# A gated linear attention and a bilinear feed-forward on one core: state products of both halves in turn, prefix sums as 64x64 tiles, and new orders

## The chip, the cores and the metric

The kernel runs on one core of a Trainium2 chip. A core has five engines with a queue of instructions each: TensorE (PE) multiplies matrices and writes to PSUM, VectorE (DVE) and ScalarE (ACT) work element by element on SBUF and PSUM, GpSimd (POOL) on SBUF alone, and SyncE (SP) issues DMAs; POOL and ACT issue DMAs too. Each queue runs in order, and the queues wait for each other through semaphores. In the profile PEld is TensorE's loading of stationary operands. The metric is the device time in microseconds (us), the median of the runs shown.

## The reference, cut to what matters

```python
state = np.zeros((B, H, D, D))                       # 4 batch rows, 8 heads, D = 48
for t in range(S):                                   # 768 tokens
    state = alpha[:, :, t, :, None] * state + np.einsum('bhd,bhe->bhde', k[:, :, t], v[:, :, t])
    y[:, :, t] = np.einsum('bhd,bhde->bhe', q[:, :, t], state)
x = y.transpose(0, 2, 1, 3).reshape(B * S, H * D)    # 3072 x 384
out = ((x @ w_a) * (x @ w_b)) @ w_out                # 384 -> 1536 -> 384
```

The recurrence decays the state by a gate per key channel. Over a block of tokens it turns into products of matrices: with b the product of the gates from the start of the block, keys divided by b and queries multiplied by b, the scores of queries and keys under a causal mask give what stays within the block, and the state that comes in gives the rest. The logarithms of the gates are summed by a matmul with a triangular matrix of ones, so b is the exponential of a prefix sum.

## The kernel before, in words

The work is six chunks. Chunk c holds two of the four batch rows (u = 0, 1) and 256 tokens (segment c // 2). Two neighbouring tokens lie on one of the 128 partitions, so the partitions hold 128 pairs. The pairs fall into two halves of 64 (g = 0, 1), that is of 128 tokens each, and the state is carried from one half to the next: S0 comes in, Sm lies between the halves, S0 of the next segment goes out.

Per chunk these steps follow each other. In brackets stand their short names in PROGRAM.

- Loads of alpha, k, q and v by DMA (ld).
- The logarithm of alpha on ACT (ln, logs), and the sum of each pair of tokens on DVE (l2, pairs, line 561).
- The prefix sums. Chunk 0 takes them straight from the logarithms in fp32 (B, cum_both). Chunks 1 to 5 split the pair sums into a high part, rounded for the fast fp32 mode (H, high, line 598), and what is left (L, low, line 604), and multiply both by the 128x128 triangle utr (A2, cum2, line 628): two matmuls of 384 columns per batch row. The triangle has zeros between the halves, so each half has sums of its own.
- The exponential of the sum and of its negative on ACT (E, line 656); products that scale keys and queries, on DVE (mk, mq, line 666); before them a product that brings the first token of a pair to its own level (lv, line 642, on POOL or DVE).
- A transpose of the scaled keys and queries, by PE and an eviction in chunks 0 and 1 (C and Ce, lines 707 to 715), by a DMA from SP afterwards (T, line 718). The decay over a half is taken from the last row of the exponentials by a pair of small DMAs (dr and dl), in chunks 0 and 1 by PE (dk and de).
- The scores, 64x64 tiles of 128 columns (D, line 786), masked on DVE (M), or copied on ACT and masked in place on DVE (Mc and Mm).
- The products of keys and values for the state, 64x64 tiles of 48 columns. K takes one half (line 744): its tiles lie in the same 64 rows of the array and take turns over its two column halves. K2 lets both halves alternate (line 757). The state is then updated on DVE (k).
- The output of attention: what is carried (SB and SA) and the inner block (Y), both at line 810, evicted as xT (X).
- The feed-forward for the chunk: a and b (line 864, 512 columns for the whole chunk, or 256 for one half of its columns), an eviction of a on ACT (as), the product with b on DVE (pr, line 878), the output matmul in two halves of six (o, line 886; oc at the very end, line 897), its eviction (ot) and the store (st).

PSUM has eight banks; the last figure of a PE step is its bank, and two-bank tiles name the first. A bank comes free when its eviction or product is done. PROGRAM is one list, written out, in which the steps of several chunks are interleaved. Each step goes to its engine's queue in the order of the list, so the list sets the order of every queue, SP's and POOL's DMAs among them. The feed-forward of one chunk fills PE while the next chunk's prefix sums, exponentials and transposes run on other engines. Two steps, fill and warm, are matmuls on zeros that only keep PE running. In the list, two further functions (cross, cum_quads) exist without being used.

Of the kernel before, what the change touches and what calls it, by code (L numbers as in the profile page):

```python
# [41 lines left out]
0: cz 1 v P
2: ld a * P
0: as 1 1; a 6 * 4; as 3 1; pr 1 1
1: ra 0
0: a 0 1 0; a 2 1 7; a 8 * 1; b 3 1 2; pr 5 1; k 1 1 V
1: H 1 V; H 0 S
0: as 6 *
1: L 1 V
0: b 2 1 3; a 11 * 5; pr 3 1  # L50
1: L 0 V
0: a 7 * 6
1: ld v 1 P
0: as 11 *; b 6 * 2; as 2 1; pr 6 *; b 11 * 7; a 10 * 4
1: ra 1
0: as 0 1; pr 2 1
1: v 0 V
0: pr 11 *; as 7 *
1: lv 0 k P; A2 0 2
2: ld k * P  # L60
0: b 0 1 0
1: A2 1 5
0: as 8 *; b 7 * 3
1: lv 0 q V
0: pr 0 1
2: ld q * P
1: E 1 i; E 0 b
0: pr 7 *
1: E 1 b; E 0 i; mq 0 V
0: b 10 * 6; b 9 * 1; a 9 * 7; as 9 *; as 10 *  # L70
1: mk 0 V
0: b 8 * 0
1: dk * 5
0: pr 8 *; pr 10 *; pr 9 *
1: C 0 1 3; C 0 0 4
0: o 3 0 0
1: Ce 0 1 S; de *; Ce 0 0 V; K2 0 7 3; D 0 0 4; k 0 0 V; D 0 1 1; Mc 0 0; lv 1 k P; SB 0 6; M 0 1
# [12 lines left out]
1: Ce 1 0 V; v 1 V  # L90
2: l2 * V
0: ot 0 S; o 1 1 -
2: ra 0
1: SA 0
0: ot 1 S
2: H * S
1: D 1 0 1; K 1 0 3
2: lv 0 k P
1: M 1 0; Y 0
0: o 2 1 -  # L100
1: X 0 S; C 1 1 5
0: ot 2 S
1: a 5 0 6
2: L * V
1: Ce 1 1 V
2: lv 1 k P
1: a 3 0 1; k 1 0 V; as 3 0; a 1 0 0; as 5 0; b 1 0 7; b 3 0 2; as 1 0
2: A2 1 1
1: pr 3 0
2: ra 1  # L110
3: ld k * P
1: pr 1 0; SB 1 5
2: E 1 i
1: D 1 1 3; K 1 1 2; M 1 1
2: lv 1 q P; lv 0 q P; E 1 b
1: a 11 0 0
2: A2 0 7
1: as 11 0; b 11 0 1
2: E 0 i
1: b 5 0 0; pr 11 0  # L120
2: E 0 b
1: a 4 0 4; pr 5 0; a 0 0 3
2: dr
1: a 6 0 1; k 1 1 V; as 4 0; as 0 0; a 2 0 0; b 4 0 7
2: mk 1 V
1: as 6 0; b 6 0 3; pr 6 0; a 7 0 1; b 0 0 2; pr 4 0; b 7 0 4; pr 0 0; a 9 0 3; as 9 0
2: mq 1 V
1: as 2 0; SA 1; Y 1; as 7 0
2: T 1
1: b 9 0 2; X 1 S; pr 7 0; a 8 0 3; pr 9 0; b 2 0 0; as 8 0  # L130
2: v 1 S
1: b 8 0 1; pr 2 0; a 10 0 4; b 10 0 2
3: lv 0 k P
1: a 0 1 0
2: mq 0 V
1: as 10 0; a 9 1 5; as 0 1; pr 10 0; a 5 1 6
4: ld a * P
1: b 5 1 7
3: ln *
1: b 0 1 3; pr 8 0; a 2 1 0  # L140
2: dl
3: lv 1 k P
1: as 5 1; pr 0 1; a 1 1 2; b 1 1 4; as 1 1; pr 5 1; as 9 1; b 9 1 3; pr 1 1; as 2 1; a 8 1 6
2: mk 0 V
1: a 4 1 7; b 2 1 1
2: v 0 S
1: as 4 1; pr 9 1; a 11 1 2; b 11 1 0; b 4 1 5; pr 2 1; b 8 1 3; pr 4 1; as 8 1; pr 8 1
3: l2 * V
1: a 3 1 4
2: T 0  # L150
1: as 11 1; a 7 1 1; b 3 1 6
0: st 3 Y
1: o 2 0 5; a 10 1 7; as 7 1
3: ld q * Y
1: pr 11 1; as 3 1
0: st 1 Y
1: as 10 1; pr 3 1
2: D 1 0 3; K * 0 1; Mc 1 0; D 1 1 6; k * 0 V
1: a 6 1 0; b 7 1 2
3: ra 1  # L160
2: Mc 1 1
1: pr 7 1
5: ld a * Y
1: b 10 1 3; o 2 1 -; as 6 1
3: ra 0
0: st 0 Y
1: b 6 1 4; ot 2 S; pr 10 1
2: Mm 1 0 V; D 0 0 2; K * 1 1
3: H * V
1: pr 6 1; o 3 0 0  # L170
2: Mc 0 0; k * 1 V; Mm 1 1 V; SB 0 4; SB 1 6
3: L * V
2: D 0 1 2
# [12 lines left out]
2: X 0 S
3: E 0 b
1: o 0 1 -
3: lv 0 q V; E 1 b; E 0 i; mk 0 V
1: ot 3 S  # L190
3: E 1 i
2: b 5 * 6; b 3 * 4; a 4 * 5; a 5 * 7
1: ot 0 S
3: mq 1 V
2: a 3 * 2; a 2 * 1
3: dr
2: a 1 * 3; as 5 *; b 0 * 7; as 3 *; b 1 * 0; as 1 *
# [36 lines left out]
2: b 10 * 5; as 9 *; a 10 * 6; b 7 * 3; pr 9 *; as 10 *; o 0 0 0; pr 7 *; pr 10 *
3: D 1 1 6; D 1 0 1
4: lv 1 k P
3: M 1 1
2: o 0 1 -
3: Mc 1 0
5: ld q * P  # L240
3: Mm 1 0 V; SB 0 3
2: ot 0 S
3: SB 1 1; D 0 1 5
4: lv 1 q V; A2 0 0
2: o 2 0 7
3: Mc 0 1
4: ra 0; lv 0 k V
5: ln *
4: E 0 b
3: Mm 0 1 V  # L250
2: o 3 0 6
3: Mm 0 0 V
5: lv 1 k P
4: lv 0 q P
5: ld v * P
3: Y 1; SA 0; Y 0; SA 1
2: o 3 1 -
3: X 0 S; X 1 V
2: o 2 1 -
4: mq 0 V; A2 1 2  # L260
2: ot 2 S
3: a 2 * 5
5: l2 * V
3: b 4 * 3
4: E 1 b; E 0 i; E 1 i
3: b 3 * 4; a 4 * 7; b 2 * 2
4: v 1 S
3: as 2 *
4: dr
# [12 lines left out]
5: lv 0 q V
3: pr 8 *
4: mq 1 V
5: lv 0 k V
3: as 0 *
5: ra 1
3: a 3 * 1; a 5 * 3; b 0 * 7; a 9 * 6; as 5 *; pr 5 *; a 7 * 3; a 11 * 5; pr 0 *; as 9 *; as 3 *; as 1 *
4: T 1
3: b 9 * 6; b 1 * 1  # L290
5: lv 1 q V
3: pr 9 *; a 6 * 2; pr 3 *; as 11 *; pr 1 *; as 6 *
4: K * 0 0; D 0 0 4
5: L * V
3: as 7 *; b 11 * 6; b 6 * 7; pr 11 *; a 10 * 1; pr 6 *
4: Mc 0 0
2: o 1 0 5
3: as 10 *
4: k * 0 V; D 1 0 3; D 1 1 6; D 0 1 1
5: v 1 S  # L300
4: Mc 1 0; M 1 1
5: A2 0 0
2: o 1 1 -
4: SB 0 6; Mc 0 1; Mm 0 0 V; SB 1 3
2: ot 1 V
5: A2 1 2
3: b 7 * 1
5: E 1 i; E 1 b; E 0 b
3: b 10 * 5
4: Mm 0 1 V; Mm 1 0 V  # L310
3: pr 7 *; o 1 0 2
5: mk 1 V
3: pr 10 *; o 2 0 1
5: mq 1 V
4: Y 1; SA 0
5: dr
2: st 3 Y
# [91 lines left out]
def kernel(  # L409
# [84 lines left out]
    def const_utr(eng):  # L494
        ENG[eng].tensor_copy(utr, ut)
# [542 lines left out]
```

## Time and profile before

| what | value |
| --- | --- |
| median of 3 runs | 195.31 us (194.95 to 195.92) |
| profiled execution, its time | 195.05 us |
| profiled execution, its span | 193.3 us |
| PE busy | 187.9 us, 97% |
| DVE busy | 132.9 us, 69% |
| ACT busy | 106.3 us, 55% |
| POOL busy | 51.4 us, 27% |
| DMA bytes | 29.40 MB, 152 GB/s over the span |

The time of an execution holds the span, from the first instruction to the last, and 1.75 us around it. Busy times are shares of the span. In the rows by slice each digit is the busy share of a fortieth of the span in tenths. The chain of work that ended last is followed back from the last instruction, at each step to what released it; its shares tell on which engine the time went. A row of the timeline gives start, length, engine, line, operation, output and inputs, shape and count; rows of the same kind that follow each other are merged. PE's matmuls overlap in the pipeline, so what one costs the queue is the distance between starts.

### The profile page before, as it was taken

How to read it: one execution, taken by the hardware profiler on the slowest of the kernel's cores; microseconds unless marked ns; L12 is line 12 of the kernel's file. 1: busy time of each engine (PE TensorE's matmuls, PEld its weight loads, DVE VectorE, ACT ScalarE, POOL GpSimd, SP SyncE). 2: the span in 40 equal slices, each digit the busy share in tenths (PEclk: the TensorE clock that was granted, in tenths of full speed). 3: DMA queues.
4: the chain of work that ended last, by engine and by line, in shares of the span. 5: the costliest groups of instructions: out<-in, count | busy, mean ns of one | idle time of the engine just before them, and what ended most of it. 6: DMA issues, size and time to landing. Idle time of an engine off the chain costs nothing.

```text
span 193.3 us, 5977 instructions
## 1 busy us (share of the span) xinstructions
PE 187.9 (97%) x2582; PEld 117.7 (61%) x2582; DVE 132.9 (69%) x221; ACT 106.3 (55%) x197; POOL 51.4 (27%) x69
## 2 busy tenths in 40 slices
PE   7989999999999999999999999999999999999993
PEld 3878875566888876644557544656455644455562
DVE  2498787988898879579787877896585525543311
ACT  4638785656859786645547775853462353431311
POOL 8999649260927003600007400000000000000000
PEclk9999999999999999999999999999999999999999
DMA  5999999999976989999598999006950100000342
GB/s 144 268 215 226 244 244 226 261 249 266 243 211 116 187 210 303 120 272 191 110 288 194 143 227 113 0 4 79 183 127 0 44 3 0 0 0 0 131 148 93
DMA packets 57034, 29.40 MB, mean 152 GB/s; under 512 B 47560, under 2 KB 54600, under 8 KB 57008
## 3 DMA queue, kind: packets, MB, share of 16 engines
q0 software_dynamic: 19056, 15.73, 44.2%
q1 hardware_dynamic: 37808, 13.19, 31.2%
q8 instruction: 20, 0.33, 0.7%
q10 hardware_dynamic: 144, 0.10, 0.2%
q14 instruction: 6, 0.05, 0.1%
HBM read 25.98 MB, written 4.74 MB: 159 GB/s over the span
## 4 chain that ended last, share of the span: by engine, by line
PE 91%; DMA 3%; POOL 2%; ACT 1%; DVE 1%; issue 1%; POOLq 0%; DVEq 0%
PE psum L864 48%; PE psum L886 24%; PE psum L810 7%; DMA a_t<-in_alpha_dram 3%; PE psum L786 3%; PE psum L628 2%; PE psum L707 2%; PE psum L744 2%; PE psum L897 1%; PE psum L687 1%; PE psum L588 1%; PE psum L589 1%; PE psum L757 1%; POOL v_t L547 0%; ACT la L554 0%
## 5 line engine op out<-in xcount | busy, mean ns | idle before, releaser
L864 PE MATMUL psum<-xT,wb_t 128*128 128x512 bf16 (+1 forms) x270 | 56.0, 337 | 0.0
L864 PE MATMUL psum<-xT,wa_t 128*128 128x512 bf16 (+1 forms) x270 | 55.5, 337 | 0.0
L886 PE MATMUL psum<-wo_t,prod 128*128 128x384 bf16 x276 | 49.5, 326 | 0.0
L864 PEld LDWEIGHTS <-wa_t 128*128 128x128 bf16 x270 | 25.9, 98 | 19.7 <-issue 0.2
L864 PEld LDWEIGHTS <-wb_t 128*128 128x128 bf16 x270 | 25.7, 98 | 20.0 <-issue 0.6
L886 PEld LDWEIGHTS <-prod 128*128 128x128 bf16 x276 | 26.0, 98 | 18.3 <-issue 0.5
L901 ACT ACTIVATE ot<-psum 128x384 f32<-128x384 f32 (+1 forms) x20 | 9.5, 480 | 19.5 <-PE psum L886 15.8
L642 POOL TENSOR_TENSOR k_t<-k_t,a_t 128x384 f32<-128x384 f32 x8 | 9.6, 1200 | 37.3 <-DMA k_t<-in_k_dram 35.9
L795 ACT ACTIVATE m<-psum 128x1024 bf16<-128x1024 f32 x15 | 15.1, 1022 | 4.6 <-PE psum L786 4.3
L791 DVE TENSOR_TENSOR m<-psum,mask 128x1024 bf16<-128x1024 f32 x9 | 10.9, 1216 | 3.2 <-PE psum L786 3.2
L554 ACT ACTIVATE la<-a_t 128x1536 f32<-128x1536 f32 (+2 forms) x9 | 9.5, 1055 | 5.6 <-DMA a_t<-in_alpha_dram 5.5
L845 ACT ACTIVATE xT<-psum 128x768 bf16<-128x768 f32 x8 | 6.5, 810 | 8.8 <-PE psum L810 8.7
L666 DVE TENSOR_TENSOR QKp<-k_t,invb 128x768 bf16<-128x768 f32 x10 | 9.4, 951 | 2.4 <-issue 1.5
L799 DVE TENSOR_TENSOR m<-m,mask 128x1024 bf16<-128x1024 bf16 x15 | 10.7, 736 | 0.1
L810 PE MATMUL psum<-m,vx 64*64 64x128 bf16 x576 | 10.2, 217 | 0.2 <-DVE m L799 0.2
L666 DVE TENSOR_TENSOR QKp<-q_t,beta 128x768 bf16<-128x768 f32 x10 | 10.0, 998 | 0.1
L786 PE MATMUL psum<-kqT 64*64 64x128 bf16 x384 | 9.7, 219 | 0.3 <-DVE kqT L715 0.2
L810 PEld LDWEIGHTS <-vx 64*64 64x64 bf16 x576 | 8.9, 107 | 1.0 <-issue 0.8
L547 POOL DMA_DIRECT2D v_t<-in_v_dram x8 | 8.4, 1051 | 0.1
L786 PEld LDWEIGHTS <-kqT 64*64 64x64 bf16 x384 | 6.7, 106 | 2.3 <-issue 1.9
L810 PE MATMUL psum<-kqT,Sm 64*64 64x128 bf16 x144 | 7.6, 220 | 0.1
L642 POOL TENSOR_TENSOR q_t<-q_t,ra 128x384 f32<-128x384 f32 x4 | 4.1, 1026 | 13.4 <-ACT m L795 13.1
(264 smaller groups left out, 281.1 us busy)
## 6 DMA issues: line engine op xcount, KB each, us to landing
out_dram<-ot SPq DMA_DIRECT2D x23, 192.0 KB, 2.9
a_t<-in_alpha_dram POOLq DMA_DIRECT2D x3, 768.0 KB, 13.8
q_t<-in_q_dram POOLq DMA_DIRECT2D x3, 768.0 KB, 8.7
k_t<-in_k_dram POOLq DMA_DIRECT2D x2, 768.0 KB, 11.7
v_t<-in_v_dram POOLq DMA_DIRECT2D x4, 384.0 KB, 6.2
k_t<-in_k_dram SPq DMA_DIRECT2D x2, 768.0 KB, 6.3
a_t<-in_alpha_dram POOLq DMA_DIRECT2D x3, 384.0 KB, 9.1
q_t<-in_q_dram POOLq DMA_DIRECT2D x3, 384.0 KB, 13.6
```

Of the source, the lines that this page charges most:

```text
L547: eng.dma_start(out=t[:, us, hs].rearrange("p b h r d -> p (b h) (r d)"), in_=src[ch.b0 + us.start:ch.b0 + us.stop, hs, ch.s * 2 * C:(ch.s ...
L554: nc.scalar.activation(out=ch.la[:, us, hs].rearrange("p b h r d -> p (b h r d)"), in_=ch.a[:, us, hs].rearrange("p b h r d -> p (b h r d) ...
L642: eng.tensor_mul(x, x, by)
L666: eng.tensor_mul(QKp[ch.c % 2][:, u, j, :, hs, :D], src[:, u, hs].rearrange("p h r d -> p r h d"), f)
L786: nc.tensor.matmul(s2[g * HC:(g + 1) * HC, r, p, rk, :], lhsT=ch.kqT[u][rs, 1, rk, 2 * h + p, g * HC:(g + 1) * HC], rhs=queriesT(ch, u, 2 ...
L791: nc.vector.tensor_mul(m.rearrange("p r a k s -> p (r a) (k s)"), ch.s2[u, h].rearrange("p r a k s -> p (r a) (k s)"), maskn(4))
L795: nc.scalar.activation(out=m.rearrange("p r a k s -> p (r a) (k s)"), in_=ch.s2[u, h].rearrange("p r a k s -> p (r a) (k s)"), func=AF.Copy)
L799: eng.tensor_mul(x, x, maskn(4))
L810: nc.tensor.matmul(y[c * DP:(c + 1) * DP, g, j // 2 * C:(j // 2 + 1) * C], lhsT=lhsT, rhs=rhs, start=(g, c) not in begun, stop=False, skip ...
L864: nc.tensor.matmul(p, lhsT=(wa_t, wb_t)[w][:, kk, f * 128:(f + 1) * 128], rhs=ch.xT[:, kk, us, :], start=(kk == 0), stop=(kk == KT - 1))
L886: nc.tensor.matmul(op, lhsT=ch.prod[:, f, at:at + C], rhs=wo_t[:, f, :], start=(f == 0), stop=(f == NFF - 1))
L901: nc.scalar.activation(out=o_, in_=i_, func=AF.Copy)
```

## The change

1. Prefix sums of chunks 2 to 5 (AQ, cum_quads in place of A2, cum2). The pair sums of batch row 1 are written to the other 64 partitions, half 0 to partitions 64 to 127 and half 1 to 0 to 63 (l2s, pairs_crossed). The sums are kept as three bf16 parts: the upper 16 bits of the fp32 sum, read in place (top), the upper 16 bits of what is left, and those of what is left again (R, rest, two differences on DVE). Twelve matmuls of 64x64 with the bf16 triangle utb and 384 columns follow: three parts by two rows by two halves, the rows in one bank each, and the four of one part in the four quarters of the array. H and L are gone for these chunks; chunk 1 keeps A2.
2. State products (K2, state_pe_both). The function now takes the batch rows of each half apart. K2 is used for both rows of chunk 1, one at a time, and for chunks 2 and 3 whole; chunk 0 and the last segment (chunks 4 and 5, where only the first half's update is needed) keep K.
3. New orders. PROGRAM is written anew throughout: which feed-forward step stands between which steps of the next chunk, the banks, the engine of some evictions, casts and level products (lv), and the order of loads and stores. In the start the fill of the first q and k tile goes from POOL to DVE, the identity is made ahead of the triangle, and SP loads k ahead of q.
4. Layouts. The decay tile and the row it comes from have the half as an inner index. Three further functions (decay_quads, decay_quads_exp, turn_quads with its eviction) are added and not used.

The diff, cut to its core (the steps of PROGRAM that the text speaks of, then the functions):

```diff
-1: A2 0 2
-1: A2 1 5
...
-2: L * V
...
-2: A2 1 1
...
-2: A2 0 7
...
-2: D 1 0 3; K * 0 1; Mc 1 0; D 1 1 6; k * 0 V
...
-2: Mm 1 0 V; D 0 0 2; K * 1 1
...
-3: A2 1 3
...
-4: lv 1 q V; A2 0 0
...
-4: mq 0 V; A2 1 2
...
-5: A2 0 0
...
-5: A2 1 2
...
+1: A2 0 7
...
+1: A2 1 7
...
+1: Mc 0 0; K2 0 0 7 0
...
+1: v 1 V; D 1 0 3; Ce 1 1 S; K2 1 1 6 0; Y 0; SA 0
...
+2: l2 0 V
+1: X 0 S; a 3 0 1; Mc 1 1
+2: l2s 0 P; l2s 1 P
+1: a 2 0 3; a 4 0 4
+2: R 0
+1: k 1 1 V; as 4 0
+2: ra 1
+1: as 3 0; b 4 0 7
+0: o 2 1 -
+1: as 2 0
+0: ot 2 S
+1: pr 4 0
+2: R 1; lv 1 q P
+1: b 3 0 6; b 2 0 7; a 5 0 2; pr 3 0; b 5 0 3; as 5 0; b 1 0 5; a 1 0 1; pr 5 0; pr 2 0; a 7 0 2; as 1 0; pr 1 0
+2: AQ 3
+1: SB 1 6
...
+2: K2 * * 0 7; D 1 1 3; D 1 0 5
...
+3: AQ 2
...
+3: K2 * * 4 6
...
+2: ot 2 S; o 0 1 -
+4: AQ 0; E 0 b; E 0 i
+3: SA 0; Y 0; SA 1
+4: E 1 b
+3: Y 1
+5: l2s 1 V
+4: mq 0 V; mk 0 V
+3: X 0 S; X 1 S
+2: o 3 0 2; o 3 1 -
+4: T 0
+3: a 5 * 3
+4: E 1 i; v 0 S
+3: a 9 * 0
+2: ot 3 S
+3: b 5 * 6; a 6 * 5; as 5 *
...
+3: a 0 * 1
+4: mk 1 V
+3: a 1 * 2
+4: D 0 0 3
...
+5: AQ 6; E 0 i; E 0 b; mk 0 V
...
-    def cross(ch, eng):
...
+    def pairs_crossed(ch, g, eng):
...
+        x = ch.la[g * HC:(g + 1) * HC, 1]
+        eng.tensor_add(ch.l2[(1 - g) * HC:(2 - g) * HC, 1], x[:, :, 0, :], x[:, :, 1, :])
+
+    def top(t):
+        return t.bitcast(BF16).rearrange("p b h (d t) -> p b (h d) t", t=2)[:, :, :, 1]
+
+    def rest(ch, n):
+        name = ("lh", "ll")[n]
+        t = wk.tile([C, 2, H, D], F32R, name=name, bufs=1)
+        setattr(ch, name, t)
+        x, hi = (ch.l2, top(ch.l2)) if n == 0 else (ch.lh.bitcast(F32), top(ch.lh))
+        nc.vector.tensor_sub(t.bitcast(F32).rearrange("p b h d -> p b (h d)"), x.rearrange("p b h d -> p b (h d)"), hi)
 
     def cum_quads(ch, i):
         p = wide(i)[:, :, :H * D]
         for u in range(2):
             ch.pf[u, 0, H] = p[:, u]
-        for t in (ch.lh, ch.ll):
+        for n, x in enumerate((top(ch.l2), top(ch.lh), top(ch.ll))):
             for u in range(2):
                 for g in range(2):
                     gs, to = slice(g * HC, (g + 1) * HC), slice((g ^ u) * HC, ((g ^ u) + 1) * HC)
-                    nc.tensor.matmul(p[to, u], lhsT=utr[gs, gs], rhs=t[gs, u].rearrange("p h d -> p (h d)"), start=(t is ch.lh), stop=(t is ch.ll))
+                    nc.tensor.matmul(p[to, u], lhsT=utb[gs, gs], rhs=x[gs, u], start=(n == 0), stop=(n == 2))
...
-    def state_pe_both(ch, us, t0, t1):
+    def state_pe_both(ch, us0, us1, t0, t1):
         i = ch.c % 2
-        for u in range(us.start, us.stop):
-            for g, tag in enumerate((t0, t1)):
+        pair = []
+        for g, us_, tag in ((0, us0, t0), (1, us1, t1)):
+            for u in range(us_.start, us_.stop):
                 ch.kv[u, g] = bank(tag)
...
+            pair.append([(u, p, rk, r) for u in range(us_.start, us_.stop) for p in range(P2) for rk in range(2) for r in range(2)])
+        for both in zip(*pair):
+            for g, (u, p, rk, r) in enumerate(both):
+                gs = slice(g * HC, (g + 1) * HC)
+                e = (u * P2 + p) * D
+                nc.tensor.matmul(ch.kv[u, g][r * DP:(r + 1) * DP, e:e + D], lhsT=QKp[i][gs, u, 1, rk, 2 * p + r, :], rhs=vxs[i][gs, u, rk, 2 * p + r, :D], start=(rk == 0), stop=(rk == 1))
```

More of the change, by code (lines that the diff above doesn't have):

```diff
@@ new lines @@
+0: pr 3 1
+1: Mc 0 0; K2 0 0 7 0
+0: o 1 0 6
+1: mk 1 V; M 0 1
+0: o 3 0 4; o 1 1 -; ot 1 S; c3 P
+3: ld a * P
+0: cs 1 0 P; o 3 1 -
+1: k 0 0 V; k 0 1 V; Mm 0 0 V; SB 0 1; C 1 0 3; C 1 1 7
+0: ot 3 S; o 0 1 -
+1: Ce 1 0 V
+2: ln *
+1: v 1 V; D 1 0 3; Ce 1 1 S; K2 1 1 6 0; Y 0; SA 0
+0: ot 0 V
+1: k 1 0 V; D 1 1 6
+0: o 2 0 5
+1: M 1 0
+2: l2 0 V
[9 more added lines that the diff above has]
+0: ot 2 S
@@ new lines @@
+2: SB 0 5
+1: pr 7 1
+3: R 0
+2: D 0 0 2
+1: ot 2 V
+2: Mm 1 0 V
+1: o 3 1 -
+2: Mc 0 0; SB 1 0; D 0 1 2
+3: R 1
+1: ot 3 S
+2: SA 0
+1: o 0 0 4
+0: cs 0 0 P
+2: Mc 0 1
+4: ln *
+3: ld q * Y; ld k * Y
+2: k * 1 V
+3: AQ 2
+2: Y 1; SA 1; Mm 0 1 V; Mm 0 0 V; Y 0; X 0 S
+3: E 0 b
+4: l2 0 V
+2: X 1 V
+1: o 0 1 -
+2: b 1 * 6; a 1 * 5
+3: E 1 b
+4: ld k * Y
+3: E 1 i
+1: ot 0 S
+3: E 0 i
+4: l2s 0 P
+2: a 0 * 0; b 0 * 1; as 0 *; as 1 *
+3: lv 0 k P; lv 0 q P
+2: a 5 * 7
+1: st 3 Y
+2: a 7 * 4
+4: l2s 1 P
@@ new lines @@
+2: a 2 * 5
+3: lv 1 q V; mq 1 V; lv 1 k V
+2: pr 1 *
+3: dr
+2: pr 0 *
+3: mk 0 V
+4: ld q * Y
+0: st 2 Y
+2: as 5 *; a 6 * 6; b 6 * 2; as 7 *
+3: mq 0 V
+2: b 9 * 4; b 7 * 0
+1: st 2 Y
+3: dl
+4: R 0
+2: b 5 * 7
+1: o 1 0 3
+2: a 9 * 1; pr 7 *; as 6 *
+3: T 0
+2: pr 6 *
+4: ra 0
+2: pr 5 *; a 11 * 6
+3: mk 1 V
+2: as 9 *; a 3 * 0
+4: lv 0 k V; lv 0 q V; R 1
+2: as 2 *
+1: o 1 1 -
+2: as 11 *; a 8 * 5; b 11 * 2; a 4 * 7; b 2 * 1
+3: T 1
+1: ot 1 V
+2: pr 9 *; as 8 *; pr 11 *; pr 2 *; b 8 * 3; b 4 * 5; as 4 *
@@ new lines @@
+5: ld v * P; lv 1 k P
+3: a 11 * 1
+5: ra 0
+3: as 3 *; pr 8 *; as 11 *; a 7 * 0
+4: D 1 0 3; K * 0 5
+5: lv 0 q P
+3: pr 3 *; as 7 *
+5: v 1 V
+4: k * 0 V
+5: R 1
+4: D 1 1 6; D 0 1 1; Mc 1 0; Mc 1 1; M 0 1
+2: o 1 0 0; o 1 1 -
+3: a 10 * 7; b 11 * 3
+4: SB 1 4
+2: ot 1 S
+3: as 10 *
+4: Mm 1 0 V
+3: pr 11 *
+4: SB 0 1
+5: AQ 6; E 0 i; E 0 b; mk 0 V
+3: b 10 * 0; b 7 * 3
+4: Mm 1 1 V
+5: mq 0 V
+3: o 2 0 6; pr 7 *
+4: Y 0; SA 0
+3: pr 10 *
+5: E 1 b
+4: X 0 V; Y 1; SA 1
+2: st 1 Y
+3: o 1 0 3
@@ new lines @@
+4: X 1 S
+3: o 2 1 -
+5: E 1 i
+4: a 7 * 2
+5: mq 1 V
+4: b 7 * 7; a 6 * 1; as 7 *; as 6 *
+3: o 1 1 -
+4: b 1 * 5; a 0 * 1; a 1 * 4
+5: dr; T 0
+2: st 3 Y
+4: b 6 * 2
+3: ot 2 V
+4: pr 7 *; a 5 * 6
+5: mk 1 V
+3: ot 1 V
+4: pr 6 *
+5: v 0 S
+4: as 0 *; as 1 *; pr 1 *
+2: st 0 Y
+5: T 1
+4: b 0 * 7; as 5 *; pr 0 *; a 4 * 1; a 3 * 0
+5: K * 0 2; dl
+4: as 4 *
+5: D 1 0 6; D 0 0 3; M 1 0
+4: as 3 *
+5: D 1 1 0; Mc 1 1; Mc 0 0; k * 0 V
+3: o 3 0 5; o 3 1 -; ot 3 S
+4: b 4 * 0; a 2 * 2
+5: SB 1 3
+4: pr 4 *
@@ new lines @@
+5: SB 0 6; D 0 1 0; M 0 1
+3: o 0 0 5; o 0 1 -
+5: Mm 1 1 V
+4: b 5 * 0
+3: ot 0 S
+4: b 3 * 1
+5: Mm 0 0 V
+4: pr 5 *; b 10 * 5; a 11 * 0
+5: SA 1; Y 1
+4: pr 3 *
+5: SA 0
+4: as 11 *
+5: X 1 S; Y 0
+4: as 2 *
+5: X 0 V
+4: a 10 * 1
+3: st 2 Y
+4: b 2 * 4; pr 2 *; b 11 * 7; as 10 *; pr 11 *; pr 10 *
+3: st 3 Y
+4: a 8 * 3
+5: b 9 * 2; a 2 * 0; b 4 * 5; a 4 * 1; b 1 * 6
+4: b 8 * 7; as 8 *
+5: as 4 *
+4: pr 8 *
+5: pr 4 *; a 8 * 4; a 1 * 3; as 2 *; as 8 *; b 8 * 0; a 11 * 5; as 1 *
+3: st 0 Y
+5: b 2 * 4; pr 1 *; pr 8 *; a 3 * 7; pr 2 *; as 11 *; a 5 * 6
```

627 lines of the change are left out of this document (237 added, 390 removed).

## The prediction

> **What bounds the kernel now.** I read the page from the top: busy shares, slices, chain of work that ended last.
>
> ```profile
> PE 187.9 (97%) x2582; PEld 117.7 (61%) x2582; DVE 132.9 (69%) x221; ACT 106.3 (55%) x197; POOL 51.4 (27%) x69
> ...
> PE   7989999999999999999999999999999999999993
> ...
> DVE  2498787988898879579787877896585525543311
> ...
> PE 91%; DMA 3%; POOL 2%; ACT 1%; DVE 1%; issue 1%; POOLq 0%; DVEq 0%
> PE psum L864 48%; PE psum L886 24%; PE psum L810 7%; DMA a_t<-in_alpha_dram 3%; PE psum L786 3%; PE psum L628 2%; PE psum L707 2%; PE psum L744 2%; PE psum L897 1%; PE psum L687 1%; PE psum L588 1%; PE psum L589 1%; PE psum L757 1%; POOL v_t L547 0%; ACT la L554 0%
> ```
>
> TensorE (PE) is the bound: 97% busy, and 91% of the chain. VectorE (DVE) is second, seven to nine tenths busy for two thirds of the run and slack after that. Since matmuls are pipelined, busy time hides small waits, so the time in stretches comes next, and then the chain in order of time, for what holds the start.
>
> ```profile
> 20.00:30.00 10.00, 9.83 (x154) 7.79 (x143) 7.78 (x20) 6.80 (x14) 5.34 (x8) 1.00 1.20 240
> ...
> 40.00:50.00 10.00, 9.92 (x210) 6.67 (x202) 8.80 (x13) 5.84 (x9) 4.79 (x5) 1.00 1.24 249
> ...
> 120.00:130.00 10.00, 10.00 (x161) 5.56 (x160) 9.47 (x15) 7.18 (x11) 0.00 (x0) 1.00 0.07 14
> ```
>
> ```profile
> 2.04 0.47 POOL QKp L511
> ...
> 2.77 0.29 POOL ut masks.py:66
> ...
> 4.22 6.69 DMA a_t<-in_alpha_dram
> 10.94 0.85 ACT la L554
> 11.83 0.59 PE psum L588 x2
> ```
>
> In the stretches (length, then PE, PEld, DVE, ACT, POOL, the granted clock at 1.00) PE lacks 0.17 and 0.08 us in two of them and nothing in the third. So after the start almost every us of PE work taken out is a us of time, and every new wait is one too. The start is held by the alpha load for row 1 of chunk 0, landing at 10.91; the logarithm and PE follow.
>
> **The change, part by part.** *Prefix sums, chunks 2 to 5.* Each batch row of a chunk now costs one cum2, two 128x384 matmuls. What it takes is the distance from its start to the next operation's start. The rows give both cases: behind small tiles, 101.85 to 102.31, 0.46; behind full ones it starts early, so the stretch is read from the first of the twelve matmuls ahead of it.
>
> ```profile
> 101.85 0.44 PE L628 MATMUL psum<-lh,utr 128*128 128x384 f32 x1
> ...
> 102.31 0.66 PE L886 MATMUL psum<-wo_t,prod 128*128 128x384 bf16 x3
> ```
>
> ```profile
> 106.17 2.12 PE L886 MATMUL psum<-wo_t,prod 128*128 128x384 bf16 x12
> 107.99 0.47 PE L628 MATMUL psum<-lh,utr 128*128 128x384 f32 x1
> ...
> 108.48 0.82 PE L864 MATMUL psum<-xT,wa_t 128*128 128x512 bf16 x3
> ```
>
> ```profile
> 76.94 1.51 PE L810 MATMUL psum<-m,vx 64*64 64x128 bf16 x96
> 78.28 0.22 PE L810 MATMUL psum<-kqT,S 64*64 64x128 bf16 x1
> ```
>
> ```profile
> 80.16 10.36 PE psum L864 x48
> ...
> 102.47 1.97 PE psum L886 x12
> 104.43 1.80 PE psum L810 x120
> ```
>
> 106.17 to 108.48 is 2.31; twelve such matmuls take 1.97 in the chain (102.47), 0.164 each; 0.34 is left for the cum2. In PROGRAM four of the eight stand behind small tiles and four behind full ones: 4 x 0.46 + 4 x 0.34 = 3.2. The new cum_quads is twelve 64x64 matmuls of 384 columns, four at a time on the four quarters. The row at 76.94 prices four quarters at once: 96 of 128 columns in 1.34, so a round of four takes 0.056, and 384 columns three times that. Three rounds are 0.50, four chunks 2.0: a saving of 1.2. Its moving operand is the upper half of each fp32, so bf16 at a pitch of 4 bytes, which no row shows. Bounds: 0.50 as above, and 1.97 if the twelve ran one after another at 0.164. I take 0.50, since the cum2 rows already read 4 bytes per column at nearly that pace.
>
> *State products.* One token half's products (L744) use two quarters of the array; with both halves alternating (L757) all four.
>
> ```profile
> 69.68 0.82 PE L864 MATMUL psum<-xT,wb_t 128*128 128x256 bf16 x6
> 70.34 1.14 PE L886 MATMUL psum<-wo_t,prod 128*128 128x384 bf16 x6
> 71.31 0.49 PE L864 MATMUL psum<-xT,wb_t 128*128 128x256 bf16 x3
> 71.73 0.42 PE L786 MATMUL psum<-kqT 64*64 64x128 bf16 x16
> 71.98 0.66 PE L744 MATMUL psum<-vx,QKp 64*64 64x48 bf16 x32
> 72.58 1.15 PE L886 MATMUL psum<-wo_t,prod 128*128 128x384 bf16 x6
> ```
>
> ```profile
> 94.34 0.70 PE L757 MATMUL psum<-vx,QKp 64*64 64x48 bf16 x64
> 94.86 0.40 PE L786 MATMUL psum<-kqT 64*64 64x128 bf16 x16
> 95.20 0.82 PE L864 MATMUL psum<-xT,wb_t 128*128 128x512 bf16 x3
> ```
>
> These rows also price a change between full and small tiles. Six 256-wide matmuls take 0.66, so three 0.33; ahead of small tiles they take 0.42 (71.31 to 71.73): 0.09 on entry. Sixteen scores take 0.25 ahead of small tiles and 0.34 ahead of full ones: 0.09 on leaving. So 32 products of one half take 0.60 - 0.09 = 0.51, 64 alternating ones 0.52. Chunk 2 saves about 0.5, row 1 of chunk 1, with half as many, at most half that, or less, since its products stand beside scores whose quarters they may share: I take 0.6 together. Chunk 3 alternated before.
>
> *New orders.* Counted in PROGRAM, PE changes between tile sizes 46 times before and 50 times after: 4 x 0.09 = 0.37 lost. Feed-forward, scores, transposes and output keep their counts; one filler fewer costs nothing, as fillers run where PE waits.
>
> *VectorE, POOL, ScalarE.* They lie beside PE.
>
> ```profile
> L642 POOL TENSOR_TENSOR k_t<-k_t,a_t x8: 987/1002/1703, 31.5 to 105.3; 128x384 f32<-128x384 f32 x8
> ```
>
> ```profile
> L604 DVE TENSOR_TENSOR ll<-l,lh 128x768 fp32r<-128x768 f32 x4 | 3.9, 968 | 0.0
> L561 DVE TENSOR_TENSOR l<-la 128x768 f32<-128x768 f32 x4 | 3.8, 950 | 0.0
> L561 DVE TENSOR_TENSOR l<-la 128x384 f32<-128x384 f32 x2 | 1.1, 558 | 0.4 <-ACT la L554 0.2
> ```
>
> Per chunk DVE had pair sums 0.95, a rounding (on ACT in chunks 2 and 5) and a difference 0.97; it gets pair sums 0.56 and two differences (rest) of 0.97: 0.58 more, 2.3 over four chunks, less the two roundings of chunks 3 and 4. DVE idles 1.2 us in the fullest 10 us of the first half (8.80) and more after 130, so this costs nothing if its queue does not block. POOL gets two 64-partition sums of about 1.0 per chunk (one goes to DVE); POOL is 27% busy. They are a new link: rest waits for both, and the feed-forward products queued behind rest on DVE wait with it. If the cover goes, PE waits for PSUM banks.
>
> *Start, loads, SP's queue, end.* On SP the k loads pass the first q load; on POOL a zero fill of 0.47 (2.04 in the chain) leaves and the identity comes ahead of the v and alpha loads, a fill and a select like the triangle's 0.29, so the alpha load that gates 11.83 is issued within 0.2 of now. Loads for chunk 1 are reordered (q first, second k between the wo loads) with the same bytes ahead. I allow 0 to 0.5, as the stretches 20 to 30 and 40 to 50 lack 0.25 now, and take 0.1. SP's decay rows and stores only move past each other. The last matmuls, eviction and store stay.
>
> *Where a chain gets short.* In chunk 4 the first scores stand much nearer their prefix sums.
>
> ```profile
> L656 ACT ACTIVATE invb<-psum 128x384 f32<-128x384 f32 x10 | 4.9, 503 | 1.0 <-PE psum L628 1.0
> ...
> L666 DVE TENSOR_TENSOR QKp<-k_t,invb 128x768 bf16<-128x768 f32 x10 | 9.4, 951 | 2.4 <-issue 1.5 <-ACT invb L656 0.9
> ```
>
> ```profile
> DMA to landing us min/median/max: 4.5/4.9/5.6
> ```
>
> Chain: one exponential 0.50, two products 0.95 each, the DMA transpose 4.5 to 5.6 to landing (second fence, tile kqT), 0.3 of handovers: 7.2 to 8.3. Cover in the new order: one inner block 1.80, twelve output matmuls 1.97, eighteen 512-wide ones at 10.36/48 = 0.216, 3.88: 7.65. PE waits 0 to 0.65; I take 0.1, as the middle of the chain, 7.75, is that much over.
>
> *Sum.* -1.2 - 0.6 + 0.37 + 0.1 + 0.1 = -1.23. The profiled execution took 195.05 (span 193.3 and 1.75 around it), 0.26 under the median 195.31; so 193.8 for it, and 194.1 for the median. What a measurement tells from no change is 0.5%, 0.98 us: below 194.33 counts as faster, above 196.29 as slower.
>
> **The rivals.** *Rows of tiles taking turns at a bank.* In cum_quads both upper and lower array halves write bank i, to opposite halves of its partitions. In L757 and L810 each array half has its own bank, so no row shows it. If they take turns, a round doubles: 1.0 per chunk, 2.0 more in all, 196.1: within the bound. The Trainium skill, page TensorEngine Tiling (Array Packing), section Gotcha 1: PSUM Pressure, says that different row tiles cannot access one PSUM bank at the same time; read strictly it speaks for this rival, and no run here shows it yet. Against it: the halves never share a partition.
>
> *POOL's sums hold VectorE (the slower side).* Place: rest of chunks 2 to 5, at the crossed sums. The L642 row has 1.70 beside a median of 1.00, so POOL adds stretch. Two at 1.70 come 1.4 late per chunk; where DVE is full, the products behind rest pass it on to PE. It decides from (196.29 - 194.1)/4 = 0.55 per chunk; at half the bound, 0.7, it adds 2.8: 196.9. Against: DVE idles 1.2 of 10 us or more, and in chunks 3 to 5 the sums can start long before they are due. The Trainium skill, page SBUF — State Buffer, section Who interferes with whom, says a VectorE instruction with two SBUF inputs contends with a GpSimd one that reads SBUF; both rest and the crossed sums are such, and the 1.70 agrees.
>
> *The twelve run alone.* 1.97 per chunk, 5.9 more: 200.0. The 96 tiles in 1.34 speak against it.
>
> **How the numbers follow.** Forecast 0.60, 193.0 to 194.8: of it 0.48 below 194.33 and 0.12 above, where the uncertain waits are nearer their upper ends. Turns at a bank 0.10, no change. POOL's sums 0.24: 0.19 slower, 0.05 stopping inside the bound. Alone 0.06, slower. Faster 0.48, same 0.27, slower 0.25. Range 193.0 to 196.9: the low end is the sum without the two waits and with 0.9 more recovered, from PE's lacking 0.25 and the rest from the start, where PE waits for loads until 11.83; the high end takes in turns and half of POOL's bound, and leaves out about 0.15.
>
> **What the changed profile would show.** Right: cum_quads rows with 0.50 to the next start; L757's successor with 192 products and 64 in 0.52; PE's first-to-last start 1 to 1.5 shorter; no PE idle at chunk 4's first scores over 0.65. Wrong: a round of four at 0.33 or twelve spaced at 0.16; DVE idle put down to POOL's sums with PE waiting for DVE behind it; PE work above 11.83 starting later.

## The result, and the profile after

The changed kernel took 193.85 us (193.53 to 193.92) against 195.41 us (194.95 to 195.92) for the kernel before in the same comparison: a ratio of 0.991, 95% interval 0.9886 to 0.9935. That is 1.6 us less. The profiled execution took 193.82 us with a span of 192.0, against 195.05 and 193.3: 1.23 less. In a second comparison, with more runs (6 of it and 17 of the kernel before), the same pair gave 0.9933 (0.9911 to 0.9954), 194.30 against 195.60.

> The changed kernel itself, beside the kernel before and the three that follow, on one chip: 1.5 us less than before (1.2 to 1.8).

It came to 1.3 us less.

First the page of the changed kernel, the parts that answer to those shown of before: busy shares, slices, chain by engine.

```profile
PE 186.8 (97%) x2613; PEld 116.9 (61%) x2613; DVE 133.1 (69%) x223; ACT 106.5 (55%) x194; POOL 56.9 (30%) x75
...
PE   7999999999999999999999999999999999999992
...
DVE  2387698994989888899897956887567446252510
...
PE 91%; DMA 5%; SPq 1%; DVE 1%; issue 1%; ACT 0%; DVEq 0%
```

PE is still the bound. POOL has 5.5 us more work, VectorE the same amount, and VectorE is fuller in the middle (36.25 us between 60 and 100, against 33.13 before). In the chain DMA went from 3% to 5%: besides a load at the start, a transpose now stands in it.

The timeline of PE in the changed kernel at chunk 2's products and at chunk 4's prefix sums (start, length, line, shape, count):

```profile
67.33 0.70 PE L812 MATMUL psum<-vx,QKp 64*64 64x48 bf16 x64
67.86 0.63 PE L841 MATMUL psum<-kqT 64*64 64x128 bf16 x32
```

```profile
102.89 0.37 PE L633 MATMUL psum<-l,utb 64*64 64x384 bf16 x4
103.08 0.34 PE L633 MATMUL psum<-lh,utb 64*64 64x384 bf16 x4
103.26 0.34 PE L633 MATMUL psum<-ll,utb 64*64 64x384 bf16 x4
103.43 0.21 PE L865 MATMUL psum<-kqT,Sm 64*64 64x128 bf16 x1
```

All 64 products of chunk 2 take 0.53 (67.33 to 67.86). The three rounds of cum_quads start 0.19, 0.18 and 0.17 apart, 0.54 in all. The four matmuls of a round, 384 columns each, run in about the 0.164 that one of the output matmuls with 384 columns takes, at a pitch of 4 bytes and with two of the four writing the same bank.

Between 100 and 150 us PE was busy all the time before; now it isn't (length, then PE, PEld, DVE, ACT, POOL, clock, of the changed kernel):

```profile
60.00:100.00 40.00, 40.00 (x605) 24.85 (x603) 36.25 (x60) 26.53 (x47) 10.71 (x10) 1.00 1.09 221
100.00:150.00 50.00, 49.71 (x750) 27.54 (x749) 36.87 (x51) 27.92 (x47) 8.55 (x8) 1.00 0.64 105
```

The missing 0.29 is one wait, at the first scores of chunk 4. These rows of the timeline and of the chain lead to it:

```profile
103.45 1.27 POOL L613 TENSOR_TENSOR l<-la 64x384 f32<-64x384 f32 x1 [1.71 <-PE psum L633]
...
104.16 1.38 DVE L678 TENSOR_TENSOR QKp<-q_t,beta 128x768 bf16<-128x768 f32 x1 [0.30 <-ACT beta L667]
105.46 0.95 DVE L678 TENSOR_TENSOR QKp<-k_t,invb 128x768 bf16<-128x768 f32 x1
...
109.11 2.11 PE L919 MATMUL psum<-xT,wa_t 128*128 128x512 bf16 x9
111.50 0.42 PE L841 MATMUL psum<-kqT 64*64 64x128 bf16 x16 [0.29 <-DMA kqT<-QKp]
```

```profile
106.47 4.99 DMA kqT<-QKp
```

Nine matmuls at 0.216 from 109.11 are through at 111.05; the scores start at 111.50, 0.45 later, of which 0.09 is the change of tile size. The q product took 1.38 us where the next three take 0.95: the sum of chunk 5 that POOL was making (103.45 to 104.72) ran beside its start, and took 1.27 itself instead of 0.99. The wait is not the same in every execution. In a second profile of the changed kernel (the run of the second comparison) the product again took 1.38, but the transpose landed after 4.82 instead of 4.99, and the scores started 2.23 behind the first of the nine matmuls instead of 2.39.

### The profile page after: what moved, and what is told of

It reads as the page before. It is cut to its first block, busy times and chain, and to the rows that moved or that the text cites. A ratio compares the mean times of both kernels' runs of the same rounds, so it can differ in the third digit from the quotient of the medians.

```text
span 192.0 us, 6086 instructions
## 1 busy us (share of the span) xinstructions
PE 186.8 (97%) x2613; PEld 116.9 (61%) x2613; DVE 133.1 (69%) x223; ACT 106.5 (55%) x194; POOL 56.9 (30%) x75
## 4 chain that ended last, share of the span: by engine, by line
PE 91%; DMA 5%; SPq 1%; DVE 1%; issue 1%; ACT 0%; DVEq 0%
PE psum L919 47%; PE psum L941 24%; PE psum L865 7%; PE psum L841 3%; DMA kqT<-QKp 3%; DMA q_t<-in_q_dram 3%; PE psum L736 2%; PE psum L633 1%; PE psum L952 1%; SPq L549 1%; PE psum L799 1%; PE psum L812 1%; PE psum L700 1%; PE psum L591 1%; PE psum L592 1%
## 5 line engine op out<-in xcount | busy, mean ns | idle before, releaser
L956 ACT ACTIVATE ot<-psum 128x384 f32<-128x384 f32 (+1 forms) x16 | 7.7, 482 | 22.7 <-PE psum L941 21.6
L850 ACT ACTIVATE m<-psum 128x1024 bf16<-128x1024 f32 x14 | 14.1, 1023 | 4.6 <-PE psum L841 4.3
L613 POOL TENSOR_TENSOR l<-la 64x384 f32<-64x384 f32 x7 | 7.8, 1108 | 26.6 <-ACT la L556 19.0
L846 DVE TENSOR_TENSOR m<-psum,mask 128x1024 bf16<-128x1024 f32 x10 | 12.1, 1220 | 3.1 <-PE psum L841 3.1
L652 POOL TENSOR_TENSOR q_t<-q_t,ra 128x384 f32<-128x384 f32 x5 | 6.1, 1215 | 22.5 <-ACT ra L645 19.7
L900 ACT ACTIVATE xT<-psum 128x768 bf16<-128x768 f32 x9 | 7.2, 816 | 5.7 <-PE psum L865 5.5
L854 DVE TENSOR_TENSOR m<-m,mask 128x1024 bf16<-128x1024 bf16 x14 | 9.3, 684 | 1.2 <-ACT m L850 1.2
L958 DVE COPY ot<-psum 128x384 f32<-128x384 f32 (+1 forms) x9 | 4.8, 532 | 7.6 <-PE psum L941 4.7
L841 PE MATMUL psum<-kqT 64*64 64x128 bf16 x384 | 9.0, 219 | 0.4 <-DMA kqT<-QKp 0.3
L652 POOL TENSOR_TENSOR k_t<-k_t,a_t 128x384 f32<-128x384 f32 x6 | 7.4, 1228 | 6.1 <-issue 3.3
## 6 DMA issues: line engine op xcount, KB each, us to landing
out_dram<-ot SPq DMA_DIRECT2D x23, 192.0 KB, 3.8
```

The costliest lines, as they stand in the source:

```text
L613: eng.tensor_add(ch.l2[(1 - g) * HC:(2 - g) * HC, 1], x[:, :, 0, :], x[:, :, 1, :])
L652: eng.tensor_mul(x, x, by)
L841: nc.tensor.matmul(s2[g * HC:(g + 1) * HC, r, p, rk, :], lhsT=turned_part(ch, u, 1, rk, 2 * h + p, g, rs), rhs=queriesT(ch, u, 2 * h + p, ...
L846: nc.vector.tensor_mul(m.rearrange("p r a k s -> p (r a) (k s)"), ch.s2[u, h].rearrange("p r a k s -> p (r a) (k s)"), maskn(4))
L850: nc.scalar.activation(out=m.rearrange("p r a k s -> p (r a) (k s)"), in_=ch.s2[u, h].rearrange("p r a k s -> p (r a) (k s)"), func=AF.Copy)
L854: eng.tensor_mul(x, x, maskn(4))
```

## The experiments

The theory at this point: both edits pay on PE what the rows priced, the new order is worth nothing or costs a little, and the 0.45 at chunk 4 comes of POOL slowing VectorE. Against it stood: the order carries the gain; POOL's sums hold VectorE; the chain at chunk 4 is simply too long.

All ratios below are to the kernel before, run beside it on the same chip, with their 95% intervals. The rows come from several such comparisons, so two rows are compared by their ratios. The state products "apart" are one token half after the other in chunks 1 and 2.

| kernel | ratio | interval |
| --- | --- | --- |
| changed kernel, first and second comparison | 0.991, 0.9933 | 0.9886 to 0.9935, 0.9911 to 0.9954 |
| new order, sums as before | 0.9943 | 0.9921 to 0.9965 |
| new order, products apart | 0.9948 | 0.9928 to 0.9969 |
| new order, sums as before, products apart | 0.9982 | 0.9967 to 0.9998 |
| changed, crossed sum later, on VectorE | 0.9924 | 0.9900 to 0.9947 |
| changed, scores later | 0.9932 | 0.9910 to 0.9954 |
| changed, crossed sums on POOL twice | 1.0033 | 1.0021 to 1.0045 |
| old order, products new | 1.0014 | 0.9994 to 1.0033 |
| old order, sums new | 1.0089 | 1.0068 to 1.0111 |
| old order, both new | 1.0147 | 1.0118 to 1.0175 |
| old order, sums new, rest later | 1.0031 | 1.0018 to 1.0045 |
| old order, rest later, chunk 2's products too | 1.0031 | 1.0015 to 1.0048 |

**Undoing one part in the new order.**

```diff
-2: l2 0 V          +2: l2 * V
-2: l2s 0 P; l2s 1 P
-2: R 0             +2: H * V
-2: R 1             +2: L * V
-2: AQ 3            +2: A2 0 3; A2 1 4        (likewise chunks 3 to 5)
```

> The changed kernel with the prefix sums of chunks 2 to 5 made as before (pair sums, rounding and difference on VectorE, two cum2 standing together where cum_quads stood); products and order as changed. If the quarters carry their part of the gain: a pair of cum2 is four matmuls at 0.164, 0.66, and with the change of tile size some 0.75, against 0.54 for cum_quads in the trace, so 0.2 more per chunk, 0.8 in all; the wait of 0.45 at chunk 4 goes, if it comes from POOL's crossed sum, which leaves 0.4 more than the changed kernel. If the gain came from the new order alone: within 0.2 of the changed kernel. If POOL's sums cost what the rival said: less time than the changed kernel.

```diff
-1: K2 0 0 7 0      +1: K 0 0 7; K 0 1 0
-1: K2 1 1 6 0      +1: K 1 0 6; K 1 1 0
-2: K2 * * 0 7      +2: K * 0 0; K * 1 7
```

> The changed kernel with the state products of chunk 1 (both rows) and chunk 2 one token half after the other, at the same places. If alternating is worth what the prediction said: chunk 2 goes from 0.53 to twice 0.48, 0.43 more; each row of chunk 1 from 0.25 to 0.38, 0.13 more; 0.7 in all. If products hide beside the scores next to them: 0.2 or less.

The start varies by some tenths from run to run, so the traces are compared over a stretch that begins behind it: from the first cum2 of chunk 1 (27.80 in the changed kernel) to the first operation behind chunk 5's prefix sums (126.64), 98.84 us. The second profile of the changed kernel gives 98.74, which shows how far such stretches repeat.

With the products apart the stretch is 27.65 to 127.34, 99.69: 0.85 more, against 0.7 expected, so alternating pays in this order. Of this 0.15 is not the edit's: row 0 of chunk 1 alternated in the kernel before too, and taking it apart moves the next operation from 0.35 to 0.50 behind its first product.

With the sums as before the stretch is 27.62 to 127.16, 99.54: 0.70 more, although the wait at chunk 4 is gone and the q product there took 0.96. A pair of cum2 side by side costs 0.88, 0.90, 0.93 and 0.82 there, cum_quads 0.54, 0.54, 0.54 and 0.61 in the changed kernel. So on PE the sums pay about 0.3 per chunk, 1.3 in all. The wait that came with them takes back about 0.36; what is left of the difference to 0.70 was not traced. By the ratios the two undoings cost 0.1 to 0.4% each; the intervals overlap with the changed kernel's.

**The wait at chunk 4.**

```diff
-5: l2s 0 P                    (beside chunk 4's first products)
+5: l2s 0 V; l2 0 V            (behind all four products)
```

> The changed kernel with one crossed sum of chunk 5 taken from POOL, where it ran beside VectorE's q product of chunk 4, and given to VectorE after both products of row 0. If the wait of PE at chunk 4's first scores is POOL slowing VectorE: the product goes from 1.38 to 0.95, the DMA transpose starts 0.43 earlier, the wait of 0.45 goes and the time falls by 0.4. If the length of the chain itself sets it: the product stays above 1.2 and the time within 0.1.

The timeline of that kernel:

```profile
104.38 0.96 DVE L674 TENSOR_TENSOR QKp<-q_t,beta 128x768 bf16<-128x768 f32 x1 [0.29 <-ACT beta L663]
...
109.33 2.11 PE L915 MATMUL psum<-xT,wa_t 128*128 128x512 bf16 x9
111.37 0.42 PE L837 MATMUL psum<-kqT 64*64 64x128 bf16 x16
```

The product takes 0.96, and the scores follow the nine matmuls after 2.04 instead of 2.39: nothing but the change of tile size is left. The kernel with the sums as before, where POOL has no sum there either, gives 2.03; the one with the products apart, which keeps POOL's sum, gives 2.50. So POOL's sum is what makes the chain too long. The time, 0.9924, can't show 0.35 us; the runs of this kernel alone lie 1.0 us apart (193.63 to 194.66).

```diff
-4: D 0 0 3
 ...
+3: b 1 * 7; 4: D 0 0 3; M 0 0
```

> The changed kernel with the first scores of chunk 4 (and their mask) behind one more feed-forward block of 0.65. If the wait there is all that is lost: 0.45 less time. If the next link is as tight (row 1's transpose, the mask behind it): the wait comes back later and the time stays within 0.15.

Here the wait only moved one block ahead. From the timeline:

```profile
109.19 2.11 PE L916 MATMUL psum<-xT,wa_t 128*128 128x512 bf16 x9
...
111.00 0.48 ACT L953 ACTIVATE ot<-psum 128x384 f32<-128x384 f32 x1
...
111.53 0.81 PE L916 MATMUL psum<-xT,wb_t 128*128 128x512 bf16 x3 [0.24 <-ACT ot L953]
```

The block that should cover the scores needs the bank that ScalarE's eviction ot frees at 111.48, so 0.40 is lost there in place of 0.45 (0.36 without the change of tile size). The scores had covered that second link. The expectation's second case held, with another link than it named.

**One part alone in the old order.** The list of before, with as few moves as the parts allow.

```diff
 (old order)
-2: l2 * V     +2: l2 0 V; l2s 0 P; l2s 1 P
-2: H * S      +2: R 0
-2: L * V      +2: R 1
-2: A2 1 1     +2: AQ 1
-2: A2 0 7                                   (likewise chunks 3 to 5; banks renamed around them)
```

> The order of before, the products as before, only the prefix sums of chunks 2 to 5 as in the changed kernel: each chunk's cum_quads where its second cum2 stood (chunk 4's two outputs later), PSUM banks renamed so that two neighbouring ones are free, both crossed sums on POOL beside the pair sums. If the sums carry the gain: cum_quads 0.54 in place of 0.46 and 0.34, less two changes of tile size that go with the second place, 1.0 to 1.4 less than before. If the order carries it: within 0.3 of before. If POOL's sums hold VectorE in an order that leaves them no room: more than before.

```diff
 (old order)
-1: K 1 0 3    +1: K2 1 1 3 0
-1: K 1 1 2
-2: K * 0 1    +2: K2 * * 0 1
-2: K * 1 1                                  (the state update moved with them; banks renamed)
```

> The order of before, the sums as before, only the state products of chunk 1's row 1 and of chunk 2 alternating, each at the place of the first half's. If alternating is worth what the prediction said: 0.6 less than before. If the second bank that they hold costs a wait: within 0.2 of before or more.

> The order of before with both edits. If the parts add up and the new order is worth nothing or a small loss, as the prediction had it: 1.7 to 2.0 less than before, 0.2 to 0.5 less than the changed kernel. If the new order is what lets the parts pay: more time than the changed kernel.

In the kernel with the sums alone and in the one with both, one feed-forward block of chunk 3 writes the bank from which another's product is still to be read, and in the former the same befalls a state update of chunk 1; that much of the result is changed, while the kinds and the number of operations are not. The mended kernels further down do not do this.

The outcome turned the theory over: put into the old order in this way, the products gain nothing (1.0014), the sums lose 0.9%, both lose 1.5%. For the sums the waits of VectorE, the waits of PE and the timeline show one place, at the crossed sums of chunk 5:

```profile
DVE lh L618 <- POOL l L608: 1.9, 1, 1.9
```

```profile
PE psum L914 <- DVE prod L928: 1.4, 2, 0.8
```

```profile
109.51 0.55 DVE L559 TENSOR_TENSOR l<-la 128x384 f32<-128x384 f32 x1
...
109.81 2.16 POOL L608 TENSOR_TENSOR l<-la 64x384 f32<-64x384 f32 x2
...
112.00 0.96 DVE L618 TENSOR_TENSOR lh<-l 128x768 f32<-128x768 f32 x1 [1.94 <-POOL l L608]
```

VectorE's rest stands in its queue and waits 1.94 us for POOL; chunk 4's k products and chunk 3's feed-forward products stand behind it, and PE waits twice for a bank. That is the path of the prediction's rival of POOL's sums, though the two sums are hardly stretched (2.16 for both): they start just behind VectorE's own part and take longer than it. The next kernel moves that one rest, and renames three banks so that no block writes one that is still to be read:

```diff
 (old order with the new sums)
-5: R 0
 ...
 4: mk 0 V
 ...
 4: mk 1 V
+5: R 0
```

> As the kernel with the sums alone in the old order, with one step moved: chunk 5's first rest stands behind chunk 4's two k products, so that VectorE no longer waits for POOL's sums in front of them (and three PSUM banks are renamed again, so that no block writes a bank that is still to be read). If POOL's sums holding VectorE there cost the 1.7 of PE's two waits behind it: 1.5 to 1.9 less than that kernel, 0.2 to 0.8 less than before. If the order of before has no room for the sums anywhere: it stays above before.

It took 1.0031, 0.6% or 1.1 us less than the kernel that it mends, and PE's two waits, 1.4 in the list above, are gone; the mechanism is shown, though the size was put at 1.5 to 1.9 and the time still lies above before's. The longest wait of PE that is left, behind the start, is in chunk 2. From its timeline, and then from that of before at the same step:

```profile
48.51 2.67 POOL L647 TENSOR_TENSOR k_t<-k_t,a_t 128x384 f32<-128x384 f32 x2 [0.30 <-DMA k_t<-in_k_dram]
...
48.73 1.58 DVE L618 TENSOR_TENSOR lh<-l 128x768 f32<-128x768 f32 x1
50.24 1.21 DVE L841 TENSOR_TENSOR m<-psum,mask 128x1024 bf16<-128x1024 f32 x1
...
51.50 0.81 PE L914 MATMUL psum<-xT,wa_t 128*128 128x256 bf16 x6 [0.79 <-DVE m L841]
```

```profile
48.13 1.22 DVE L791 TENSOR_TENSOR m<-psum,mask 128x1024 bf16<-128x1024 f32 x1 [0.65 <-PE psum L786]
```

Before, the rounding of chunk 2 ran on ScalarE, and the mask followed the scores at 48.13. With the new sums a rest stands there on VectorE, drawn out to 1.58 beside POOL's level product, and the mask starts at 50.24; PE waits 0.79 for its bank. The changed kernel has the mask first (47.98) and the rest behind it. No run moved this rest alone, so what it costs in time is not shown.

> The old order with the sums (the first rest of chunk 5 moved as in the run above) and chunk 2's products alternating; chunk 1's row 1 as before. If the parts then add up: 0.4 less than the run above, 0.8 to 1.3 less than before, near the changed kernel. If VectorE's queue, fuller by the rests, is late elsewhere: within 0.4 of before.

With chunk 2's products as well it stays at 1.0031, 0.6 above before: neither case held, and the second, within 0.4, is the nearer. In the kernel with the products alone the timeline shows where their gain goes, at row 1 of chunk 1:

```profile
48.11 0.49 ACT L956 ACTIVATE ot<-psum 128x384 f32<-128x384 f32 x1 [1.16 <-PE psum L941]
...
48.27 0.18 PE L812 MATMUL psum<-vx,QKp 64*64 64x48 bf16 x1
...
48.65 0.43 PE L812 MATMUL psum<-vx,QKp 64*64 64x48 bf16 x31
```

Alternating needs the second half's bank as soon as the first's. In this list that is bank 0, which holds an output of chunk 0 until ScalarE's eviction ends at 48.60, so the second product starts 0.38 behind the first. The bank then stays taken until VectorE's update of the state has read it, and a feed-forward block of chunk 1 needs it next. In the kernel with both edits, where VectorE is later, this second wait is long:

```profile
54.17 0.49 PE L914 MATMUL psum<-xT,wb_t 128*128 128x256 bf16 x3 [1.05 <-DVE tmp L824]
```

That is the second case of the expectation for the products: the second bank that they hold costs a wait. It is read from the timeline; no run changed the bank alone, and where the gain of chunk 2's products goes in the mended kernel was not traced.

**The order alone, and the room for POOL.** The order alone is the new list with both undoings shown above; the new start and the layouts are in it too.

> The new order with both edits undone: sums as before (the two cum2 side by side where cum_quads stood), products one half after the other in chunks 1 and 2. If the order itself costs, as the prediction had it (four more changes of tile size, 0.37, and early waits): 0.2 to 0.6 more than before. If the order carries part of the gain: 0.3 or more less than before, and the sum of the two single undoings (0.2 to 0.4, and 0.6 to 0.8) gives it back.

It took 0.9982, 0.35 us less than before by the ratio: not the loss of 0.2 to 0.6, and by a little the second case, a part of the gain. It is little against the interval (0.9967 to 0.9998), and the profiled executions do not show it (a span of 193.5 against 193.3). Since this kernel also takes apart row 0 of chunk 1, 0.15 in the trace, the order alone may be worth somewhat more.

With the two undoings (0.9943, 0.9948) and the changed kernel this makes a square. In the new order each edit alone brings 0.3 to 0.4% and both bring 0.5 to 0.7%; put into the old order each brings nothing or a loss. The stretch from chunk 1's first cum2 to the end of chunk 5's prefix sums gives the same square for the new order: 100.13 (28.14 to 128.27) with both undone, 99.69 with the new sums alone, 99.54 with the new products alone, 98.84 with both. So both edits together are worth 1.29 there, 0.15 of it from row 0 of chunk 1; the sums bring 0.44 to 0.70 and the products 0.59 to 0.85, by whether the other edit is in.

```diff
-2: l2s 0 P; l2s 1 P
+2: l2s 0 P; l2s 0 P; l2s 1 P; l2s 1 P        (likewise on POOL in chunks 3 to 5)
```

> The changed kernel with each of the seven crossed sums on POOL issued twice (7 us more work on POOL). If the new order leaves them room: in chunk 2 the rest, which now starts 0.95 after POOL's second sum, comes 1.05 late, in chunks 3 and 4 it has more room than that, and at chunk 4's first scores VectorE's two products are both slowed, 0.45 more wait; 0.5 to 1.3 more than the changed kernel in all. If POOL is already what holds VectorE: 2 more per chunk, 5 or more in all. If POOL's sums touch nothing: within 0.3.

It took 1.0033, by the ratios about 2 us more than the changed kernel, above the 0.5 to 1.3 expected. First the changed kernel's rows at chunk 2, then those of this one:

```profile
46.75 2.05 POOL L613 TENSOR_TENSOR l<-la 64x384 f32<-64x384 f32 x2 [5.76 <-issue]
...
49.76 0.96 DVE L623 TENSOR_TENSOR lh<-l 128x768 f32<-128x768 f32 x1
```

```profile
46.82 4.39 POOL L609 TENSOR_TENSOR l<-la 64x384 f32<-64x384 f32 x4 [5.43 <-issue]
...
51.24 0.96 DVE L619 TENSOR_TENSOR lh<-l 128x768 f32<-128x768 f32 x1 [0.89 <-POOL l L609]
...
53.68 0.49 PE L915 MATMUL psum<-xT,wb_t 128*128 128x256 bf16 x3 [1.28 <-DVE prod L929]
```

In the changed kernel POOL ends at 48.80 and the rest starts at 49.76: 0.96 of room. Past that room nearly all of the delay reaches PE, 1.28 for a rest that is 1.48 later, and the wait at chunk 4 grows to 0.8 in this kernel's list of waits (PE for the DMA of kqT). So the rival that the prediction put at 0.24 was about one us of POOL's time away.

## Why the prediction was right, and where not

The time, 193.85, lies 0.25 under the 194.1 forecast and in the likeliest case's own range, 193.0 to 194.8. The sum was right to the profiled execution (1.23 forecast, 1.23 measured), but partly by luck, because errors met: the edits paid 1.29 in the stretch, waits included, less than the 1.6 left of the -1.8 after the two waits of 0.1, and the order, put at +0.37, took 0.35 off.

- **Prefix sums, -1.2.** Forecast 0.50 for cum_quads, measured 0.54, and 0.61 where a feed-forward block follows. Against cum2 side by side in the new order that is 1.3 less PE time, against the 3.2 that the prediction gave the cum2 of before it is 1.0. The price on PE was right, but undoing the sums costs only 0.44 to 0.70 in the stretch: the price on VectorE and POOL, put at nothing, was not nothing, and a part stays open.
- **State products, -0.6.** 64 alternating ones take 0.53, and undoing what the change added costs 0.44 to 0.70 in the new order (0.59 to 0.85, less 0.15 for the row that alternated before). Right.
- **New orders, +0.37.** This is the step that failed. It counted changes of tile size and took the order for a cost beside two gains. The order alone costs nothing (0.9982), and in the old order, with the fewest moves, the gains do not come (1.0014, 1.0031, 1.0031). The prediction did write that VectorE's extra work costs nothing "if its queue does not block"; whether it blocks, and whether a second bank is free for the products, is what the order decides, and the step gave that no number. Whether a better place for the edits in the old order would have brought the gain was not tried.
- **Chunk 4's first scores, +0.1.** Measured 0.45, 0.36 without the change of tile size (0.29 and 0.20 in the second profile). The chain was 8.03 (103.43 to 111.46), near the top of the 7.2 to 8.3 given; the sum took 7.75. What it lacked is 0.43 by which POOL slows the q product.
- **Early waits, +0.1.** Not seen: between 20 and 60 us PE now lacks nothing, where it lacked 0.25 before. The work that the prediction gives as starting at 11.83 starts at 12.03, one of its signs of being wrong; but it lies between 11.54 and 12.03 in runs with the same start, so this decides nothing.
- **Turns at a bank, and twelve alone.** Both fall: rounds of four start 0.17 to 0.19 apart, neither 0.33 apart nor with 0.16 for each matmul. The Trainium skill, page TensorEngine Tiling (Array Packing), section Gotcha 1: PSUM Pressure, says that different row tiles cannot access one bank at the same time. Here two row tiles write to the two partition halves of one bank and lose nothing, so for this case the measurement decides.
- **POOL's sums hold VectorE.** It did not decide here, but it exists: VectorE waits 1.94 for POOL in the old order, and 0.89 with the sums doubled. The prediction let it decide from 0.55 late per chunk, and at chunk 2 the rest had 0.96 of room before it would be late at all. The Trainium skill, page SBUF — State Buffer, section Who interferes with whom, says that a VectorE instruction with two SBUF inputs contends with a GpSimd one that reads SBUF. The traces agree: 1.38 beside POOL and 0.96 without, 1.58 for a rest of 0.95. Not every overlap shows it, though: VectorE's own crossed sum at 103.31 in the changed kernel lay beside POOL's for 0.42 and still took 0.56.

## What to carry to other kernels

Where one engine is the bound, price an edit on it from start-to-start distances, but then ask for each new step on the other engines what stands behind it in its queue, and how long before it is due its input is ready. An edit and the order that it is put in are one change: with an order that leaves 1 us of room in front of the new wait edits and order gained 0.7 to 0.9%, the edits alone 0.5 to 0.7%; in one without that room the sums lost 0.3 to 0.9%. A product that alternates between two banks needs both free at once, which is a wait to look for as well. When a wait is moved away, look for the next link at the same place before counting the gain.

## What the runs showed of the hardware

- Twelve 64x64 matmuls of 384 columns, with the upper bf16 halves of fp32 words as moving operand, take 0.54 us; two row tiles that write different partition halves of one bank do not slow each other: a round of four takes 0.17 to 0.19, and the prediction's rows, where each half has a bank of its own, gave 0.17.
- A sum over 64 partitions takes POOL as long as a product over 128 with the same 384 columns (0.99 and 0.99 undisturbed), and VectorE too (0.56 and 0.55), so splitting a sum by partitions doubles its cost. These sums write to the other 64 partitions, which adds nothing that the times show.
- Beside each other VectorE's 0.95 became 1.38 to 1.58, and POOL's 0.99 became 1.27. With POOL's sums doubled, a VectorE product took 1.74 beside them.
